# One quarter of the last block's gate by half products beside another stage, and three row sums by negated copies and DMA

## The chip, the cores and the metric

The kernel runs on one core of a Trainium2 chip. The metric is the device time of one execution in microseconds. Three runs of the kernel before gave 201.1, 200.7 and 201.03, a median of 201.03. The profile is of one execution; times within it count from its first instruction, and its span goes to the last one.

## The reference

A sequence of 2048 tokens of width 512 is normalized, and two branches of the normalized sequence are added to the input: a diagonal state space model with 512 complex states, and a gated unit of width 1792.

```python
xn  = (x - mean(x)) / sqrt(var(x) + 1e-5)              # x: [1, 2048, 512], bf16
Bu  = einsum("bld,pd->blp", xn, B_bar)                 # 512 complex states
h_t = Lam_bar * h_(t-1) + Bu_t                         # a scan over the 2048 tokens
A   = 2 * einsum("blp,dp->bld", h, C).real + xn * Dskip
Bo  = (silu(xn @ w1) * (xn @ w3)) @ w2                 # w1, w3: [512, 1792], w2: [1792, 512]
out = x + A + Bo
```

## The kernel before

**Blocks, chunks, pairs.** The 2048 tokens are four blocks (0 to 3) of 512, each of four chunks of 128. Two chunks of a block are a pair; pairs 0 to 7 run through the blocks, so pair 4 is the first half of block 2, pair 5 its second half, pairs 6 and 7 are block 3. TensorE is given its work in a fixed order: gate and up projections of a block (`glu`, and `glu_last` for block 3), the state inputs (`bu`, or `bu_fast` by half products), and the output products of the pairs (`y_fast`).

**The activation tile.** `act(b)` holds for each chunk of a block the left operands of the output product, fp16, as 22 slices of 128x128: 14 products silu(gate) * up, and 8 slices of states. The first 11 (`NK`) are the first seven gate slices and the states of the first half of the state space, the other 11 the rest. A pair thus has four quarters `a11`, `a12` (its first chunk) and `a21`, `a22` (its second).

**Seven products for eight.** `y_fast(n)` computes the two output chunks of a pair with Strassen's seven products in Winograd's form, each eleven matmuls of 256 columns (L1054). Its left operands are the quarters and four sums, made by `row_sums(n)`: `s3 = a11 - a21`, `s2 = s3 - a22`, `s1 = a21 + a22` (in place of `a21`) and, inside `y_fast`, `s4 = a12 + s2` (in place of `a12`, L1093 by an accumulating transfer that GpSimd issues, or L1096 by VectorE). `s2` and `s3` have homes in old tiles: for even pairs in the first two blocks of `x_all`, for odd ones in the last quarter of `tw`. The order of the products of pair 4 is 1, 4, 2, 6, 5, 7, 3. Product 3, which reads `s4`, is put off for the pairs in `LATER`: for pair 4 it runs inside pair 5, behind product 5, and for pair 5 inside pair 6.

`glu_last(3)` takes the 14 feature slices of block 3 so: slices 12 and 13 first, plainly; then three groups (`NG`) of four slices. In a group the up projection is computed by seven products (`product`, L869: four matmuls of 256 columns each) whose left operands are quarters of `w3` and their sums over weights (`up_sums`, `ups`), and whose right operands are quarters and column sums of the block's normalized input (`t1` to `t4`). The gate projection is computed plainly by `gate_side` (L848: four matmuls of 512 columns for a slice), four of these to a group, set between the products. Of a group's PSUM tiles two are `ps_y` banks (`g`, `e`) and two `ps_bu` banks (`f`, `z`); each of the two pools has two banks. ScalarE copies one running sum into the next bank (L857) and `silu`s the gate sides (L860); VectorE adds the copied product `s5` to two of the quarters (L879); each pair of slices ends with silu(gate) * up on VectorE (L864). The sum `s4` of each group is made on VectorE at L910.

**VectorE's queue.** The work that need not stand at a fixed place is queued in `Filler`: each task has a planned cost, the planner keeps a planned time for TensorE (`tensor`) and for VectorE, and `fill` issues tasks while VectorE's planned time plus half of the next task's cost is within TensorE's planned time plus a lead (1.7). `own` books fixed work. `flush(key)` issues everything up to the last task with that key. `y_fast` opens with flushes: its own pair's sums, and, for the first pair of block 2 or 3, the scans of the next block's first half:

```python
        bg.flush(("sums", n))
        bg.flush("tw")
        bg.flush(("difference", b))
        if p == 0 and b > 1:
            bg.flush(("scan", b + 1))
```

The queue at the point of the change holds, in this order, the rest of block 2's state products, block 3's products ahead of its scans (`pre_a`, `pre_b`, `pre_c` for each half), pair 4's row sums, the four scans of block 3's first half (`scans0`, L505), and what follows from these. `pre_c` adds a product to the state input: on VectorE at L493, or by an accumulating transfer at L495.

Instructions on one engine run in the order in which the program issues them, and GpSimd (POOL) issues the accumulating transfers in its own order.

Of the kernel before, what the change touches and what calls it, by code (L numbers as in the profile page):

```python
# [63 lines left out]
def kernel(  # L64
# [31 lines left out]
    NG = 3  # L96
    TH = TBLK // 2
    LEAD = 1.7
    LATER = (4, 5)
    AHEAD = (MID, 8, 1, None)  # L100
    NWARM = 10
    DH = D // 2
# [359 lines left out]
    def ssm_tasks(b, posts_last=False, between=(), middle=(), late=()):  # L462
# [5 lines left out]
        def half(hf):  # L468
            psl = slice(2 * hf, 2 * hf + 2)
            st = {}  # L470

            def pre_a():
                if b == 0:
                    sin_step((2 * hf + 1, 1))
                    nc.vector.tensor_scalar(out=tabe[:, psl, 2, :], in0=tabe[:, psl, 1, :], scalar1=-1.0,
                                            scalar2=None, op0=ALU.mult)
                st["g"] = u_blk[b, hf]
                if (b, hf) == (3, 0):
                    st["p"] = up.tile(FULL, BF16, name="u")
                elif b == NBLK - 1:  # L480
                    st["p"] = xtp.tile([P, NDT, TBLK], BF16, name="xnT").rearrange("p (j r) t -> p j r t", r=2)
                else:
                    st["p"] = ssmw.tile(FULL, BF16, name="p")
                nc.vector.tensor_tensor(out=st["p"][:, :, ::-1, :], in0=st["g"], in1=tabe[:, psl, 2:0:-1, :],
                                        op=ALU.mult)

            def pre_b():
                nc.vector.tensor_tensor(out=st["g"], in0=st["g"], in1=tabe[:, psl, 0:1, :].to_broadcast(FULL),  # L488
                                        op=ALU.mult)

            def pre_c():
                if b == 0 or (b, hf) == (2, 0):
                    nc.vector.tensor_tensor(out=st["g"], in0=st["g"], in1=st["p"], op=ALU.add)  # L493
                else:
                    gp.dma_start(out=st["g"], in_=st["p"], accum_op=ALU.add)  # L495

            def scan(j, ri):
                pt = 2 * hf + j
                init = 0.0
                if b in (1, 2):  # L500
                    init = ends[:, hf, 2 * j + ri:2 * j + ri + 1]
                elif b > 2:
                    init = act_blk[b - 1][:, CPB - 1, k_state(pt, ri), P - 1:P]
                v = st["g"][:, j, ri, :]
                nc.vector.tensor_tensor_scan(out=v, data0=rho[:, pt:pt + 1].to_broadcast([P, TBLK]), data1=v,  # L505
                                             initial=init, op0=ALU.mult, op1=ALU.add)

            def post_a(csl=slice(0, CPB)):
                if "p16" not in st:
                    st["p16"] = ssmw.tile(FULL, BF16, name="p").bitcast(FP16).rearrange(  # L510
                        "p j r (c t) -> p (j r c t)", t=P).rearrange("p (c k t) -> p c k t", c=CPB, t=P)
                tsl = slice(csl.start * P, csl.stop * P)
                nc.vector.tensor_tensor(out=by_state(st["p16"][:, csl]), in0=by_chunk(st["g"][:, :, ::-1, tsl]),  # L513
                                        in1=by_chunk(tabe[:, psl, 2:0:-1, tsl]), op=ALU.mult)

            def post_b(csl=slice(0, CPB)):
                tsl = slice(csl.start * P, csl.stop * P)
                n = csl.stop - csl.start
                nc.vector.tensor_tensor(out=by_state(act_state(b, hf)[:, csl]), in0=by_chunk(st["g"][:, :, :, tsl]),  # L519
                                        in1=by_chunk(tabe[:, psl, 0:1, tsl]).to_broadcast([P, 2, 2, n, P]), op=ALU.mult)  # L520

            def post_c(csl=slice(0, CPB)):
                a, p16 = act_state(b, hf)[:, csl], st["p16"][:, csl]
                if b == NBLK - 1 and (hf == 1 or csl.start > 0):
                    nc.vector.tensor_tensor(out=a, in0=a, in1=p16, op=ALU.add)
                else:
                    gp.dma_start(out=a, in_=p16, accum_op=ALU.add)  # L527

            if (b, hf) == (1, 1):
                pre_c.ready = lambda: ("squares", 2, CPB - 1) in sins_done  # L530
            pre_a.ready = lambda: (b, hf) in u_blk
            scans = [lambda j=j, ri=ri: scan(j, ri) for j in range(2) for ri in range(2)]
            return (pre_a, pre_b, pre_c), scans, (post_a, post_b, post_c)

        (pre0, scans0, post0), (pre1, scans1, post1) = (half(hf) for hf in range(NPT // 2))

        transfers = (post0[2],) + (() if b == NBLK - 1 else (post1[2],)) + ((pre1[2],) if b > 0 else ()) + ((pre0[2],) if b in (1, 3) else ())

        def add(*fns):
            for fn in fns:  # L540
# [285 lines left out]
    def up_sums(b):  # L826
# [8 lines left out]
                for out, x, z, op in ((s1, a21, a22, ALU.add), (s3, a11, a21, ALU.subtract),  # L835
                                      (s2, s1, a11, ALU.subtract))]

    def glu_last(b):
        xnT = xnT_blk[b]
        s1, s2, s3, s4 = ups["s"]  # L840
# [33 lines left out]
        def halves(ps):  # L874
            return ps.rearrange("p (h t) -> p h t", h=2)

        def add(out, ps):
            bg.own(0.7)
            nc.vector.tensor_tensor(out=out, in0=halves(ps), in1=halves(s5), op=ALU.add)  # L879

        gates = []
        for f in range(4 * NG, NFT):
            if f % 2 == 0:
                tiles = pair_tiles()
            gate_side(f, tiles[0])
            copy(tiles[1][:, f % 2, :], side(w3_sb, f))
            bg.fill()
            if f % 2 == 0 and gates:
                gates.pop()()
            if f % 2 == 1:  # L890
                gates.append(lambda f=f, tiles=tiles: gate(f - 1, tiles))
        for n in range(NG):
            f0 = 4 * n
            a11, a12, a22, s1n, s2n, s3n, s4n = (v[:, :, n, :] for v in (
                up_quarter(0, 0), up_quarter(1, 0), up_quarter(1, 1), s1, s2, s3, s4))
            g, e = (ps_y.tile([P, TBLK], FP32, name="y_ps") for _ in range(2))
            f, z = (ps_bu.tile([P, TBLK], FP32, name="bu_ps") for _ in range(2))
            upper, lower = pair_tiles(), pair_tiles()
            product(g, a11, b11, True)
            copy(f, g)  # L900
            product(e, s1n, t1, True)
            copy(s5, e)
            gate_side(f0, upper[0])
            bg.fill(0.8)
            gates.pop()()
            product(f, a12, b21, False)
            product(g, s2n, t2, False)
            copy(e, g)
            bg.own(0.42)
            nc.vector.tensor_tensor(out=s4n, in0=a12, in1=s2n, op=ALU.subtract)  # L910
            copy(upper[1][:, :, 0:TH], halves(f))
            gate_side(f0 + 1, upper[0])
            bg.fill()
            product(g, s3n, t3, False)
            copy(z, g)
            add(lower[1][:, :, TH:TBLK], g)
            product(e, s4n, b22, False)
            add(upper[1][:, :, TH:TBLK], e)
            gate_side(f0 + 2, lower[0])
            bg.fill()  # L920
            gate(f0, upper)
            product(z, a22, t4, False)
            copy(lower[1][:, :, 0:TH], halves(z))
            gate_side(f0 + 3, lower[0])
            bg.fill()
            gates.append(lambda f0=f0, lower=lower: gate(f0 + 2, lower))
        seeds(4)
        return gates.pop()


    def res_list(b):
# [56 lines left out]
        return [[v[:, 0:n] for v in xs], [spare[:, 0:n], spare[:, n:2 * n]]], q  # L988

    sums = {}  # L990

    def row_sums(n, b, p):
        a = act(b)
# [5 lines left out]
        def subtract(out, x, z):  # L999
            return lambda: nc.vector.tensor_tensor(out=out, in0=x, in1=z, op=ALU.subtract)  # L1000

        three = (0.84, subtract(s3, a11, a21), ("sums", n))
        two = (0.84, subtract(s2, s3, a22), ("sums", n))
        if n in (1, 6, 7):
            one = (0.84, lambda: nc.vector.tensor_tensor(out=a21, in0=a21, in1=a22, op=ALU.add), ("sums", n))
        else:
            one = (0.0, lambda: gp.dma_start(out=a21, in_=a22, accum_op=ALU.add), ("sums", n))
# [28 lines left out]
    def y_fast(n, then=(), between=()):  # L1036
# [50 lines left out]
        def product2():  # L1087
# [9 lines left out]
            add(o1[:, D1], f, o1[:, D1])  # L1097
            if last:
                store(c1, o1, D1)
            if n + 1 < len(pairs) and n not in (1, 2, 3) and n - 1 not in LATER:  # L1100
                seeds(n + 1)
            steps()

# [43 lines left out]
        for i in ((1, 5, 2, 6, 4, 3, 7) if b == 0 else (1, 2, 4, 6, 5, 7, 3) if b == 1 else ORDER.get(n, (1, 4, 2, 6, 5, 7, 3))):  # L1147
# [10 lines left out]
            if between:  # L1158
# [2 lines left out]
                    bg.fill()  # L1161
                if n == 3 and not between:
                    bg.first(up_sums(3))
            if n == 2 and i == 7:
                seeds(3)

    ln_alloc(0)
    ln1a, ln1b = ln_tasks_vector(1)
# [70 lines left out]
    y_done.append(2)  # L1239
    y_fast(3, (), bu_fast(3, 1))  # L1240
    bg.flush("up")
    gate = glu_last(3)
    gate()
    for n in range(4, len(pairs)):
        ahead = row_sums(n + 1, *pairs[n + 1]) if n + 1 < len(pairs) else ()
        if n > 4:
            for t in ahead:
                bg.add(*t)
        if n == 5:
            for t in (difference(3), *last_posts):  # L1250
                bg.add(*t)
        y_fast(n, ahead if n == 4 else ())


# [28 lines left out]
```

## Time and profile before

| | |
|---|---|
| median of three runs | 201.03 us (200.7 to 201.1) |
| span of the profiled execution | 199.5 us |
| TensorE matmuls busy | 195.6 us (98%), 1401 instructions |
| VectorE busy | 181.8 us (91%), 254 instructions |
| ScalarE busy | 135.0 us (68%), 281 instructions |
| GpSimd busy | 51.5 us (26%), 75 instructions |
| `glu_last(3)` on TensorE | 140.05 to 163.10 us |
| pairs 4 and 5 on TensorE, with product 3 of pair 4 but not of pair 5 | 163.10 to 178.71 us |
| pairs 6 and 7, with product 3 of pair 5 | 178.71 to 196.79 us |

The page gives the profiled execution's span and no separate time for it. Busy time is per engine; an engine that is busy all the time is the bound only where the others wait for it. The chain of waits follows the execution back from its last instruction, and the timeline lists one engine's instructions by start, with the duration and, in brackets, the idle time before one and what ended it. Durations of neighbouring instructions overlap a little, so the distance between two starts is the better measure of what an instruction adds.

### The profile page before, as it was taken

Reading aid. Unit: us, or ns where it says so; the run is one execution under the profiler, and the core shown is the slowest. Engines: PE = TensorE matmul, PEld = TensorE weight load, DVE = VectorE, ACT = ScalarE, POOL = GpSimd, SP = SyncE. Lnnn points to the kernel's source line nnn. Section 1 sums busy time; section 2 is a strip of 40 time slices with the busy share of each in tenths; the row PEclk is TensorE's granted clock in tenths of the full one; section 3 lists DMA queues with packets and bytes.
Section 4 is the critical chain, followed back from the end, with each engine's and each line's share of the span. In section 5 each row is a group of like instructions: output and inputs, shape, how many; then the busy total and the mean of one; then the engine's idle time right before and its main releaser. Section 6 shows DMA issues by size and latency. Waiting matters only on the chain.

```text
span 199.5 us, 3700 instructions
## 1 busy us (share of the span) xinstructions
PE 195.6 (98%) x1401; PEld 130.7 (65%) x1401; DVE 181.8 (91%) x254; ACT 135.0 (68%) x281; POOL 51.5 (26%) x75
## 2 busy tenths in 40 slices
PE   8999999999999999999999999999999999999994
PEld 2774444444444488866555468888566678888893
DVE  3689699999999999989999997999999999999972
ACT  4699897699999996968998684362588783111220
POOL 7180289700411134041202305040021303310000
PEclk9999999999999999999999999999999999999999
DMA  4999996991497054730997455838137732941111
GB/s 138 326 277 200 302 186 124 343 273 23 69 181 141 0 105 82 135 105 0 156 148 119 89 92 98 172 83 132 53 59 129 149 56 52 174 92 36 53 44 40
DMA packets 32258, 25.12 MB, mean 126 GB/s; under 512 B 16240, under 2 KB 29936, under 8 KB 32240
## 3 DMA queue, kind: packets, MB, share of 16 engines
q0 software_dynamic: 6128, 11.38, 33.5%
q1 hardware_dynamic: 25536, 13.21, 26.8%
q10 hardware_dynamic: 576, 0.30, 0.5%
q8 instruction: 11, 0.18, 0.4%
q14 instruction: 7, 0.06, 0.1%
HBM read 7.74 MB, written 2.10 MB: 49 GB/s over the span
## 4 chain that ended last, share of the span: by engine, by line
PE 95%; DMA 2%; SPq 1%; issue 0%; DVE 0%
PE gu_ps L587 34%; PE gu_ps L1054 17%; PE y_ps L1054 10%; PE gu_ps L848 7%; PE bu_ps L1054 7%; PE bu_ps L454 3%; PE y_ps L454 3%; PE y_ps L869 3%; PE y_ps L780 3%; DMA w_sb<-in_B_w_dram 2%; PE gu_ps L619 2%; PE gu_ps L780 2%; PE bu_ps L869 1%; PE bu_ps L780 1%; PE bu_ps L619 1%; SPq L166 0%
## 5 line engine op out<-in xcount | busy, mean ns | idle before, releaser
L587 PE MATMUL gu_ps<-xnT,w_sb 128*128 128x512 bf16 x312 | 69.6, 379 | 0.0
L587 PEld LDWEIGHTS <-w_sb 128*128 128x128 bf16 x312 | 30.5, 98 | 34.2
L1054 PEld LDWEIGHTS <-act 128*128 128x128 f16 x462 | 43.5, 98 | 5.4
L596 ACT ACTIVATE g<-gu_ps 128x512 bf16<-128x512 f32 x41 | 24.8, 606 | 6.0 <-PE gu_ps L587 3.6
L597 ACT ACTIVATE u<-gu_ps 128x512 bf16<-128x512 f32 x41 | 24.8, 606 | 4.5 <-PE gu_ps L587 3.7
L505 DVE TENSOR_TENSOR_SCAN u<-rho,ends,u 128x512 bf16<-128x512 f32 x16 | 20.0, 1270 | 0.0
L527 POOL DMA_DIRECT2D act<-p x7 | 9.2, 1320 | 34.0 <-DVE act L519 22.1
L1054 PE MATMUL gu_ps<-w_sb,act 128*128 128x256 bf16 (+3 forms) x126 | 16.0, 267 | 0.0
L848 PE MATMUL gu_ps<-xnT,w_sb 128*128 128x512 bf16 x64 | 15.9, 379 | 0.0
L604 DVE TENSOR_TENSOR act<-g,u 128x1024 f16<-128x1024 bf16 x21 | 14.2, 679 | 0.4 <-ACT u L597 0.4
L860 ACT ACTIVATE g<-gu_ps 128x512 bf16<-128x512 f32 x14 | 8.4, 599 | 5.4 <-PE gu_ps L848 5.0
L454 PEld LDWEIGHTS <-bt 128*128 128x128 bf16 x64 | 6.3, 98 | 7.5
L1077 ACT ACTIVATE x_blk<-gu_ps 128x256 f32<-128x256 f32 (+1 forms) x9 | 3.3, 368 | 10.6 <-PE gu_ps L1054 10.6
L1054 PE MATMUL bu_ps<-w_sb,act 128*128 128x256 bf16 (+3 forms) x84 | 10.4, 264 | 0.0
L1054 PE MATMUL gu_ps<-ct,act 128*128 128x256 f16 (+1 forms) x72 | 10.4, 267 | 0.0
L848 PEld LDWEIGHTS <-w_sb 128*128 128x128 bf16 x64 | 6.3, 98 | 4.8
L505 DVE TENSOR_TENSOR_SCAN u<-rho,u 128x512 bf16<-128x512 f32 x8 | 9.2, 1206 | 0.0
L1054 PEld LDWEIGHTS <-x_blk 128*128 128x128 f16 x88 | 8.6, 98 | 1.0
L1054 PEld LDWEIGHTS <-tw 128*128 128x128 f16 x88 | 8.6, 98 | 1.0
L513 DVE TENSOR_TENSOR p<-u,tabe 128x2048 f16<-128x2048 bf16 (+1 forms) x8 | 8.7, 1085 | 0.1
L519 DVE TENSOR_TENSOR act<-u,tabe 128x2048 f16<-128x2048 bf16 (+1 forms) x8 | 8.7, 1083 | 0.0
L488 DVE TENSOR_TENSOR u<-u,tabe 128x2048 bf16<-128x2048 bf16 x7 | 8.5, 1219 | 0.1
(203 smaller groups left out, 392.5 us busy)
## 6 DMA issues: line engine op xcount, KB each, us to landing
act<-p POOLq DMA_DIRECT2D x6, 512.0 KB, 6.1
xn<-x_blk POOLq DMA_DIRECT2D x4, 512.0 KB, 5.5
out_dram<-xn SPq DMA_DIRECT2D x15, 128.0 KB, 1.7
w_sb<-in_B_w_dram SPq DMA_DIRECT2D x1, 1792.0 KB, 8.2
act<-act POOLq DMA_DIRECT2D x5, 352.0 KB, 4.6
w_sb<-in_B_w_dram SPq DMA_DIRECT2D x2, 768.0 KB, 6.4
u<-p POOLq DMA_DIRECT2D x3, 512.0 KB, 5.1
w_sb<-in_B_w_dram SPq DMA_DIRECT2D x4, 256.0 KB, 4.9
```

Source lines behind the costliest of these rows:

```text
L454: nc.tensor.matmul(out=ps, lhsT=bt[:, ri, dt, pt * P:(pt + 1) * P], rhs=xnT_blk[b][:, dt, :], start=(dt == 0), stop=(dt == NDT - 1))
L505: nc.vector.tensor_tensor_scan(out=v, data0=rho[:, pt:pt + 1].to_broadcast([P, TBLK]), data1=v, initial=init, op0=ALU.mult, op1=ALU.add)
L513: nc.vector.tensor_tensor(out=by_state(st["p16"][:, csl]), in0=by_chunk(st["g"][:, :, ::-1, tsl]), in1=by_chunk(tabe[:, psl, 2:0:-1, tsl]) ...
L519: nc.vector.tensor_tensor(out=by_state(act_state(b, hf)[:, csl]), in0=by_chunk(st["g"][:, :, :, tsl]), in1=by_chunk(tabe[:, psl, 0:1, tsl] ...
L527: gp.dma_start(out=a, in_=p16, accum_op=ALU.add)
L587: nc.tensor.matmul(out=ps[:, tsl], lhsT=w[:, dt, f * P:(f + 1) * P], rhs=xnT[:, dt, tsl], start=(dt == 0), stop=(dt == NDT - 1))
L596: nc.scalar.activation(out=g16[:, f % 2, :], in_=g_ps, func=ACT.Silu)
L597: nc.scalar.activation(out=u16[:, f % 2, :], in_=u_ps, func=ACT.Copy)
L604: nc.vector.tensor_tensor(out=act_gates(b, f - 1), in0=split(g16), in1=split(u16), op=ALU.mult)
L780: nc.tensor.matmul(out=out[:, h * TH:(h + 1) * TH], lhsT=left[:, h, k, :], rhs=right[:, k, :], start=(start and h == 0 and k == 0), stop=( ...
L848: nc.tensor.matmul(out=ps, lhsT=w[:, dt, f * P:(f + 1) * P], rhs=xnT[:, dt, :], start=(dt == 0), stop=(dt == NDT - 1))
L1054: nc.tensor.matmul(out=out, lhsT=left[:, k, :], rhs=right[k][:, cols], start=(start and k == 0), stop=(k == NK - 1), skip_group_check=True)
```

## The change

For the third group of `glu_last(3)` (slices 8 to 11) the gate side is no longer computed by four plain projections set between the up side's products. It is computed by seven half products of its own, with the same right operands, and both sets of seven run beside pair 4: `glu_last` issues the up side's first two products and returns the rest as six steps, which `y_fast(4)` takes between its products. The gate side's left operands are quarters of `w1`; their five sums (`gate_sums`) are made on VectorE during groups 0 and 1, in the places of the first two groups' old sums, and the up side's own `s4` of that group with them. Where a gate quarter needs the added `s5`, VectorE adds it in the PSUM bank, and ScalarE's silu then reads the bank.

Three row sums, `s3` of pair 4 and `s3` and `s2` of pair 5, are no longer made on VectorE. ScalarE writes a negated copy of the second operand, and GpSimd issues a transfer that adds the first. `pre_c` of block 2's first half goes from VectorE to a transfer. Pair 4 leaves `LATER`, so its product 3 stands in its place in the order, and pair 5's PSUM tiles are seeded behind pair 4's product 7.

```diff
-    LATER = (4, 5)
+    LATER = (5,)
...
             def pre_c():
-                if b == 0 or (b, hf) == (2, 0):
+                if b == 0:
                     nc.vector.tensor_tensor(out=st["g"], in0=st["g"], in1=st["p"], op=ALU.add)
                 else:
                     gp.dma_start(out=st["g"], in_=st["p"], accum_op=ALU.add)
...
+    def gate_quarter(kh, r, half=False):
+        f0 = 4 * (NG - 1) * P
+        v = w1_sb[:, 2 * kh:2 * kh + 2, f0 + r * 2 * P:f0 + (r + 1) * 2 * P]
+        return v.bitcast(FP16) if half else v
+
+    def gate_sums():
+        s1, s2 = (ups["s"][i][:, :, 0, :] for i in range(2))
+        a11, a12, a21, a22 = (gate_quarter(*i) for i in ((0, 0), (1, 0), (0, 1), (1, 1)))
+        s3 = gate_quarter(0, 1, True)
+        u2 = ups["s"][1][:, :, NG - 1, :]
+        u4, s4 = (ups["s"][i][:, :, 1, :] for i in range(2))
+        ups["gs"] = a11, a12, a22, s1, s2, s3, s4
+        ups["u4"] = u4
+        return [(0.42, lambda out=out, x=x, z=z, op=op: nc.vector.tensor_tensor(out=out, in0=x, in1=z, op=op), "gs")
+                for out, x, z, op in ((s1, a21, a22, ALU.add), (s3, a11, a21, ALU.subtract),
+                                      (s2, s1, a11, ALU.subtract))], [
+            (0.42, lambda out=out, x=x, z=z: nc.vector.tensor_tensor(out=out, in0=x, in1=z, op=ALU.subtract), "gs")
+            for out, x, z in ((u4, up_quarter(1, 0)[:, :, NG - 1, :], u2), (s4, a12, s2))]
...
+        def group(lefts, four, top, low, gated):
+            a11, a12, a22, s1n, s2n, s3n, s4n = lefts
+            g, e = (ps_y.tile([P, TBLK], FP32, name="y_ps") for _ in range(2))
+            f, z = (ps_bu.tile([P, TBLK], FP32, name="bu_ps") for _ in range(2))
+
+            def end(out, ps):
+                nc.scalar.activation(out=out, in_=halves(ps), func=ACT.Silu if gated else ACT.Copy)
+
+            def add(out, ps):
+                bg.own(0.7)
+                nc.vector.tensor_tensor(out=halves(ps) if gated else out, in0=halves(ps), in1=halves(s5), op=ALU.add)
+                if gated:
+                    end(out, ps)
+
+            def one():
+                product(g, a11, b11, True)
+                copy(f, g)
+
+            def five():
+                product(e, s1n, t1, True)
+                copy(s5, e)
+
+            def two():
+                product(f, a12, b21, False)
+
+            def six():
+                product(g, s2n, t2, False)
+                copy(e, g)
+                four()
+                end(top[:, :, 0:TH], f)
+
+            def seven():
+                product(g, s3n, t3, False)
+                copy(z, g)
+                add(low[:, :, TH:TBLK], g)
+
+            def three():
+                product(e, s4n, b22, False)
+                add(top[:, :, TH:TBLK], e)
+
+            def last():
+                product(z, a22, t4, False)
+                end(low[:, :, 0:TH], z)
+
+            return one, five, two, six, seven, three, last
...
         gates = []
+        by_copy[4][0][0]()
...
-        for n in range(NG):
+        for n in range(NG - 1):
...
+            one()
+            five()
+            by_copy[5][0][n + 1]()
...
+            if n == 1:
+                bg.first(sums_b)
+                bg.flush("gs")
+            if n == 0:
+                sums_a, sums_b = gate_sums()
+                bg.first(sums_a)
         seeds(4)
-        return gates.pop()
...
+        one, five, two, six, seven, three, last = up_steps
+        gone, gfive, gtwo, gsix, gseven, gthree, glast = (gate_step(i) for i in range(7))
+        first = gates.pop()
+        return (one, five, by_copy[5][1][1], first), deque(((two, six, by_copy[5][1][2]), (seven, three), (last, gone, gfive), (gtwo, gsix),
+                                          (gseven, gthree), (glast, lambda: gate(f0, upper), lambda: gate(f0 + 2, lower))))
...
+        def from_copy(out, x, z, k0, k1, transfer):
+            nc.scalar.activation(out=out[:, k0:k1], in_=z[:, k0:k1], func=ACT.Copy, scale=-1.0)
+            if transfer:
+                gp.dma_start(out=out, in_=x, accum_op=ALU.add)
+
+        KH = (NK + 1) // 2
+        by_copy[n] = [[lambda v=v, r=r, k=k: from_copy(*v, *r, k) for r, k in (((0, NK), True), ((0, KH), False),
+                                                                              ((KH, NK), True))]
+                      for v in ((s3, a11, a21), (s2, s3, a22))]
...
+        if n in (4, 5):
+            three = (0.0, lambda: None, ("sums", n))
+        if n == 5:
+            two = (0.0, lambda: None, ("sums", n))
...
-            if n + 1 < len(pairs) and n not in (1, 2, 3) and n - 1 not in LATER:
+            if n + 1 < len(pairs) and n not in (1, 2, 3, 4) and n - 1 not in LATER:
                 seeds(n + 1)
...
-            if n == 2 and i == 7:
-                seeds(3)
+            if n in (2, 4) and i == 7:
+                seeds(n + 1)
...
-    gate = glu_last(3)
-    gate()
+    sums5 = row_sums(5, *pairs[5])
+    begin, beside = glu_last(3)
+    for step in begin:
+        step()
+        bg.fill()
...
-        y_fast(n, ahead if n == 4 else ())
+        y_fast(n, ahead if n == 4 else (), beside if n == 4 else ())
```

The steps of the up half keep the group's old names (`one` to `last`); those of the gate half are `gone`, `gfive`, `gtwo`, `gsix`, `gseven`, `gthree` and `glast`. `group` for the gate half is called with its first step, and so takes the PSUM banks that the up half has had.

## The prediction

> **What bounds the kernel now.** I read the page's chain of waits first, then that chain in order of time around the change, then VectorE's timeline over the same stretch, because an engine that is not the bound can still hold the one that is.
>
> ```profile
> PE 95%; DMA 2%; SPq 1%; issue 0%; DVE 0%
> ```
>
> TensorE is 95% of the chain. In order of time, the third tile group of block 3 (the one that the change touches) and the pair behind it, as start, duration and what ran:
>
> ```profile
> 156.56 0.87 PE y_ps L869 x8
> 157.43 0.86 PE gu_ps L848 x4
> 158.30 0.44 PE bu_ps L869 x4
> 158.73 0.44 PE y_ps L869 x4
> 159.17 0.86 PE gu_ps L848 x4
> 160.03 0.90 PE y_ps L869 x8
> 160.93 0.86 PE gu_ps L848 x4
> 161.80 0.44 PE bu_ps L869 x4
> 162.23 0.86 PE gu_ps L848 x4
> 163.10 7.21 PE gu_ps L1054 x66
> ```
>
> Every piece starts where the last one ended: TensorE waits for nobody here, so work taken from it shortens the run by its own size, provided that no wait appears. Four 512-column matmuls take 0.865 us (157.43 to 158.30), four 256-column ones 0.436 (0.87 for eight), and a product of a pair, eleven matmuls, 1.20 (7.21 for 66).
>
> VectorE over the same stretch:
>
> ```profile
> 154.83 1.29 DVE L879 TENSOR_TENSOR u<-y_ps,bt 128x512 bf16<-128x512 f32 x2 [0.31 <-ACT bu_ps L857]
> 156.03 0.88 DVE L1000 TENSOR_TENSOR x_blk<-act 128x1408 f16<-128x1408 f16 x1
> 156.83 0.68 DVE L864 TENSOR_TENSOR act<-g,u 128x1024 f16<-128x1024 bf16 x1
> 157.44 0.88 DVE L1000 TENSOR_TENSOR x_blk<-x_blk,act 128x1408 f16<-128x1408 f16 x1
> 158.24 0.68 DVE L864 TENSOR_TENSOR act<-g,u 128x1024 f16<-128x1024 bf16 x1
> 158.84 0.42 DVE L910 TENSOR_TENSOR w_sb<-w_sb,bt 128x512 f16<-128x512 bf16 x1
> 159.18 2.45 DVE L505 TENSOR_TENSOR_SCAN u<-rho,act,u 128x512 bf16<-128x512 f32 x2
> 161.55 1.26 DVE L879 TENSOR_TENSOR u<-y_ps,bt 128x512 bf16<-128x512 f32 x2
> 162.84 0.69 DVE L864 TENSOR_TENSOR act<-g,u 128x1024 f16<-128x1024 bf16 x1
> 163.45 1.28 DVE L505 TENSOR_TENSOR_SCAN u<-rho,act,u 128x512 bf16<-128x512 f32 x1
> 164.65 0.67 DVE L864 TENSOR_TENSOR act<-g,u 128x1024 f16<-128x1024 bf16 x1
> 165.23 1.28 DVE L505 TENSOR_TENSOR_SCAN u<-rho,act,u 128x512 bf16<-128x512 f32 x1
> ```
>
> VectorE is as full as TensorE: it goes from row to row without a gap, and it is late. The two adds of the third group (161.55) start 1.1 us after the product that the first of them reads has ended (160.03 + 0.44); that harms nobody here, since no matmul wants those PSUM banks soon. The four scans of block 3's first half are spread over 159.18 to 166.4, with the adds and gates between them. Starts differ by less than the durations, so I use start-to-start: 0.80 for a 1408-wide row sum, 0.60 for an add or a gate product, 0.34 for a 512-wide sum, 1.19 for a scan.
>
> **The change, part by part.** TensorE loses four gate sides, 4 x 0.865 = 3.46, and gains seven half products, 7 x 0.436 = 3.05: **-0.41 us**. All the rest is moved. If nothing waited, that would be the whole effect.
>
> VectorE loses the 2048-wide add of block 2 (1.14: 107.73 to 108.87 in its timeline), three row sums (3 x 0.80 = 2.40) and the third group's own sum (0.34); it gains five sums of the gate quarters (5 x 0.34 = 1.70) and two PSUM adds (2 x 0.60). Over the whole run that is -0.98, so VectorE as an average gets lighter. What matters is when.
>
> The block 2 add becomes a POOL transfer issued near 108. The like rows (L495) take 0.9 to 1.5 us on POOL and land 4.5 to 7.4 us after issue, so by 115.5; the scan that reads it stands at 121.58. On POOL it stands ahead of the residual transfer (111.23) and pair 2's row sum (113.05); a delay of that one by up to 3 us still lands by about 121, ahead of its product at 124.5. I price it at nothing; without that cover it would be up to 6 us on VectorE (7.4 less 1.14).
>
> The three row sums become ScalarE copies with a POOL accumulate. No row shows a 1408-wide copy. Bounds: 0.60 (a 512-wide one) and 1.96 (the 0.712 of a scaled 512-wide one times 2.75); the straight line through 0.38 at 256 and 0.60 at 512 gives 1.37, which I take, and 0.82 for the half of 768. The first fits into ScalarE's 2.6 us of idling before 140.95. A half beside group 0 starts the copy that frees PSUM for the next product some 0.1 late, against 0.2 of room (146.77 to 146.97): nothing, at worst 0.1. The Trainium skill, "ScalarE: Activation LUTs", section "Rules for kernel authors", speaks against this: such arithmetic belongs on VectorE. The same page's 186 + 0.833 N ns would make the copy 1.36 us by an estimate, as against 0.88 for the row sum; the sum here is the same by either, as ScalarE isn't on the path.
>
> The accumulates are 352 KB, as the row sums' own (0.86 on POOL, landing after 3.8 to 5.2). Pair 5's second waits on POOL for the first to land; behind it stands pair 4's fourth sum, a transfer that can start after its second product (162.8) and lands by 166.6 to 168.5. Pair 4's third product, no longer put off to pair 5, reads it at about 169.9. It costs nothing by that; the worst landing of such a tile in the trace, 9.1, would cost about 2.0, less whatever TensorE has already waited.
>
> **The wait that is new** is in the order. The gate half's products reuse the two ps_y banks of the up half's. The first of them may start only when VectorE's add in step `seven` has read the first bank, the second when the add in `three` has read the other. When does TensorE want them? From 156.56: one and five 0.87, pair product 1.20, two and six 0.87, pair product 1.20, seven and three 0.87, pair product 1.20, last 0.44: **163.21**.
>
> When is VectorE there? y_fast(4) opens by flushing pair 4's sums and block 3's four scans. Before, that call stood at 163.1 on TensorE and found only one scan left. Now it stands after two products of the third group, at 157.43, and all four scans are still queued: walking the queue's own arithmetic (limit TensorE + 1.7, next task's half cost) through groups 0 and 1, no scan is taken earlier. So all four are issued ahead of both adds. Start from 156.03, where the adds of group 1 end; their start, 154.83, is held by a ScalarE copy, so that the 1.14 saved at 107 is largely used up in such waits. Then the second row sum of pair 4 (0.80), two gates (1.20), the last two gate sums (0.68), four scans (2.37 x 2 = 4.74), the add (0.66 to its end): 156.03 + 0.80 + 1.20 + 0.68 + 4.74 + 0.66 = **164.11**. TensorE waits 0.90. The second bank is free 0.60 later, at 164.71, while `gone` ends at 164.55: another 0.16. **Stall 1.06**, and I take 1.1 with the tenth by which the copy ahead of group 1's adds is late.
>
> Bounds for the stall: if the saved 1.14 survives up to a row sum's worth, 0.3; if one more 2048-wide product of the queue (1.14) falls behind the adds at 154.83 and not into the 0.31 gap before them, 1.9. I take 1.1, since 154.83 is held from outside.
>
> Later the sum doesn't change: the nearest edge on VectorE behind is the last block's state add, which ends 189.37 before its product at 189.51, 0.14 of room. TensorE comes 0.7 later there and VectorE has two row sums fewer to do, so the room grows.
>
> **Sum.** The profiled execution's span is 199.5; the runs' median is 201.03, so 1.53 lies around the span, as I leave it. 199.5 - 0.41 + 1.1 = 200.2, and with 1.53 **201.7 us**. A difference of 0.2% (0.40 us) is about what a measurement of this kernel can tell from none.
>
> **Rivals.**
> - *No stall: 200.6.* 201.03 - 0.41. For it: VectorE's total falls by 0.98 and 1.14 of it well ahead. It decides if the four scans are through by 162.5, 0.9 earlier than I have them. Against it: the gaps at 148.3 and 154.8 are waits for ScalarE, which no lighter queue shortens. Even whole, it only just reaches 0.2%.
> - *Half a stall: 201.0.* VectorE arrives 0.7 ahead of my sum, the stall is 0.4 and eats the gain.
> - *A late transfer as well: 202.6.* Pair 4's fourth sum lands 9.1 after 162.8 and holds the third product for 0.9 beyond the 1.1. For it: two or three accumulates now share POOL's queue between 155 and 165. The Trainium skill, "DMA: Bandwidth & Descriptors", section "Two DMAs through the same engine are not ordered", has the issuing engine wait for the first one's completion; pair 5's second accumulate stands so on POOL. Against it: the two like rows with x_blk at 120.7 and 167.0 landed in 3.8, and the stall itself gives it a microsecond more.
>
> **How the numbers follow.** Stall 0.70, half 0.15, none 0.10, late transfer too 0.05. The stall's own range is 201.3 to 202.2 (0.7 to 1.6 of stall). For 8 in 10 I go down to 200.8, into the half case, and up to 202.5, the upper bound of the stall. Slower by over 0.2% needs a stall above 0.81: most of the first case and the last, less the edge: 0.70. Within 0.2%: 0.18. Faster: 0.12, the case without stall and its neighbours, as its middle lies on the edge.
>
> **What would show it.** The chain should have a gap or a DVE piece near 163 to 164, of about 1 us, ahead of the gate half's first product, with four scans in a row on VectorE before it; L869's matmuls 28 more, L848's 16 fewer; ScalarE copies of 1.3 to 1.4 us; pair 4's third product without a wait. I am wrong if TensorE goes through 157 to 172 without a gap, if the scans stand ahead of 158, or if a gap is elsewhere: in group 0's `three`, where the sum before it (146.36) may slip by up to 0.2, or ahead of pair 4's third product.

## The result and the profile after

The changed kernel takes 202.69 us (median of six runs, 202.28 to 203.26) against 201.06 (200.7 to 201.13) for the kernel before in the same comparison. The ratio is 1.0081, with a 95% interval of 1.0065 to 1.0096: **slower by 1.6 us**, where 201.7 with a range of 200.8 to 202.5 was forecast.

The page of the changed kernel, the line of the chain that was first read before:

```profile
PE 84%; DMA 6%; DVE 4%; ACT 2%; issue 1%; SPq 1%
```

TensorE was 95% of the chain. Transfers and VectorE now stand in it, so TensorE waits, and the chain in order of time says where (start, duration, what ran or was waited for):

```profile
132.16 0.76 DMA act<-p
132.91 6.57 DMA act<-tw
139.48 0.05 issue
139.52 1.38 PE bu_ps L1152 x11
...
159.70 4.72 DVE u L505 x4
164.43 0.59 DVE u L906
165.02 0.04 issue
165.06 1.19 PE y_ps L888 x8
```

There are two places. (Line numbers have moved: L1152 is the pair products' L1054, L888 the half products' L869, L906 the adds' L879, L1191 the fourth sum's transfer L1093.) The second is the wait of the prediction: four scans in a row, then the add, then the gate half's first product. The first place was not forecast: **pair 3's last product, well ahead of the changed stage, waits for a transfer**. TensorE's own timeline shows both, with the idle time in brackets:

```profile
137.77 1.36 PE L1152 MATMUL y_ps<-tw 128*128 128x256 f16 x11
139.52 0.94 PE L1152 MATMUL bu_ps<-w_sb,act 128*128 128x256 bf16 x7 [0.39 <-DMA act<-tw]
...
165.06 0.60 PE L888 MATMUL y_ps<-xnT,w_sb 128*128 128x256 bf16 x4 [0.93 <-DVE u L906]
165.66 0.60 PE L888 MATMUL y_ps<-x_blk,bt 128*128 128x256 f16 x4
```

A pair product is 1.20 us from start to start, so pair 3's third would have begun at 138.97: it is 0.55 late (the brackets count less, since the busy time of a matmul is drawn past the next one's start). By the timeline, where the third group's first product starts at 157.31, the gate half's first would have started 6.65 us behind it (the forecast's 163.21 less 156.56), at 163.96: it is 1.10 late. The second starts 0.60 behind the first where the next set follows after 0.44 in a running sequence, another 0.16. So 1.26 is lost there. (On the chain the same loss falls into other parts, because in a running sequence the chain places a product 0.16 behind its start in the timeline, and behind a wait it doesn't: 157.47 + 6.65 = 164.12, so 0.94 for the wait, and 0.32 for the two products, 1.19 in place of 0.87.)

From the first product of pair 3 to the start of VectorE's last instruction, on the chain, the kernel before takes 68.23 us (128.58 to 196.81) and the changed one 69.68 (128.87 to 198.55): +1.45, against -0.41 + 0.55 + 1.26 = 1.40. What lies ahead of pair 3 differs by 0.29 in these two executions. The first load of weights takes 4.95 and 4.53 us on the chain, and part of that difference is made good just behind it. Pair 3 starts anywhere between 128.10 (e5) and 129.08 (e1) in the profiles of the changed kernel and of its variants below, so this start is scatter, and all that follows counts from pair 3.

VectorE at the end of group 1, then where the adds come:

```profile
155.74 1.29 DVE L906 TENSOR_TENSOR u<-y_ps,bt 128x512 bf16<-128x512 f32 x2 [0.31 <-ACT bu_ps L876]
156.94 0.88 DVE L1085 TENSOR_TENSOR x_blk<-x_blk,act 128x1408 f16<-128x1408 f16 x1
157.74 0.69 DVE L883 TENSOR_TENSOR act<-g,u 128x1024 f16<-128x1024 bf16 x1
158.34 0.76 DVE L854 TENSOR_TENSOR bt<-w_sb,bt 128x512 f16<-128x512 bf16 x2
159.01 0.69 DVE L883 TENSOR_TENSOR act<-g,u 128x1024 f16<-128x1024 bf16 x1
159.62 4.81 DVE L505 TENSOR_TENSOR_SCAN u<-rho,act,u 128x512 bf16<-128x512 f32 x4
164.34 1.27 DVE L906 TENSOR_TENSOR u<-y_ps,bt 128x512 bf16<-128x512 f32 x2
```

These are the terms of the forecast sum, one by one: a row sum, a gate, two gate sums, a gate, four scans, the adds.

### The profile page after: what moved, and what is told of

Its sections match the earlier page's. It is cut to its first block, busy times and chain, and to the rows that moved or that the text cites. A ratio compares the mean times of both kernels' runs of the same rounds, so it can differ in the third digit from the quotient of the medians.

```text
span 201.3 us, 3737 instructions
## 1 busy us (share of the span) xinstructions
PE 195.3 (97%) x1400; PEld 132.3 (66%) x1413; DVE 180.7 (90%) x256; ACT 140.4 (70%) x290; POOL 55.3 (27%) x79
## 4 chain that ended last, share of the span: by engine, by line
PE 84%; DMA 6%; DVE 4%; ACT 2%; issue 1%; SPq 1%
PE gu_ps L587 33%; PE gu_ps L1152 16%; PE y_ps L1152 8%; PE bu_ps L1152 6%; PE bu_ps L454 3%; PE y_ps L454 3%; PE gu_ps L867 3%; DMA act<-tw 3%; PE y_ps L780 3%; DMA w_sb<-in_B_w_dram 2%; PE y_ps L888 2%; DVE u L505 2%; PE gu_ps L619 2%; PE bu_ps L780 1%; PE bu_ps L888 1%
## 5 line engine op out<-in xcount | busy, mean ns | idle before, releaser
L587 PE MATMUL gu_ps<-xnT,w_sb 128*128 128x512 bf16 x304 | 68.9, 379 | 0.4
L587 PEld LDWEIGHTS <-w_sb 128*128 128x128 bf16 x312 | 30.5, 98 | 34.2
L1152 PEld LDWEIGHTS <-act 128*128 128x128 f16 x462 | 43.5, 98 | 5.8 <-DMA act<-tw 0.7
L596 ACT ACTIVATE g<-gu_ps 128x512 bf16<-128x512 f32 x41 | 24.8, 606 | 6.2 <-PE gu_ps L587 3.3
L527 POOL DMA_DIRECT2D act<-p x7 | 9.1, 1306 | 38.6 <-DVE act L519 24.2
L1152 PE MATMUL gu_ps<-w_sb,act 128*128 128x256 bf16 (+3 forms) x126 | 16.0, 267 | 0.0
L867 PE MATMUL gu_ps<-xnT,w_sb 128*128 128x512 bf16 x45 | 11.5, 379 | 0.1
L1152 PE MATMUL bu_ps<-w_sb,act 128*128 128x256 bf16 (+3 forms) x84 | 10.4, 264 | 0.4 <-DMA act<-tw 0.4
L1152 PE MATMUL gu_ps<-ct,act 128*128 128x256 f16 (+1 forms) x72 | 10.4, 267 | 0.0
L888 PEld LDWEIGHTS <-w_sb 128*128 128x128 bf16 (+1 forms) x72 | 7.0, 98 | 3.9 <-issue 1.3
L1152 PEld LDWEIGHTS <-x_blk 128*128 128x128 f16 x88 | 8.6, 98 | 1.0
L1152 PEld LDWEIGHTS <-tw 128*128 128x128 f16 x88 | 8.6, 98 | 1.0
L879 ACT ACTIVATE g<-gu_ps 128x512 bf16<-128x512 f32 x10 | 6.0, 599 | 3.6 <-PE gu_ps L867 3.1
```

The costliest lines, as they stand in the source:

```text
L587: nc.tensor.matmul(out=ps[:, tsl], lhsT=w[:, dt, f * P:(f + 1) * P], rhs=xnT[:, dt, tsl], start=(dt == 0), stop=(dt == NDT - 1))
L596: nc.scalar.activation(out=g16[:, f % 2, :], in_=g_ps, func=ACT.Silu)
L867: nc.tensor.matmul(out=ps, lhsT=w[:, dt, f * P:(f + 1) * P], rhs=xnT[:, dt, :], start=(dt == 0), stop=(dt == NDT - 1))
L888: nc.tensor.matmul(out=out[:, h * TH:(h + 1) * TH], lhsT=left[:, k, h * P:(h + 1) * P], rhs=right[:, k, :], start=(start and h == 0 and k ...
L1152: nc.tensor.matmul(out=out, lhsT=left[:, k, :], rhs=right[k][:, cols], start=(start and k == 0), stop=(k == NK - 1), skip_group_check=True)
```

## The experiments

Each kernel is the changed one with the edit shown, if nothing else is said. The kernel before ran beside them: 201.21 us in the batch of e1 to e4, 201.0 in that of e5 to e8.

**e1: the order of block 2, by the planner's booking.** The added transfer of block 2 is booked as if VectorE still did the work, so that the queue's order is that of the kernel before.

```diff
-((pre0[2],) if b > 0 else ())
+((pre0[2],) if b in (1, 3) else ())
```

> The changed kernel with one thing altered: the planner goes on booking 1.16 us for block 2's addition to its state input, which is still a transfer. VectorE's order is then that of the kernel before up to block 3, and on POOL pair 3's fourth sum is issued ahead of block 2's state transfer again. Theory (the order on POOL made pair 3's third product wait 0.55 us): that wait is gone, the transfer lands about 3.8 us after issue and not 6.6; the wait of the gate half's first product (1.1 + 0.16) stays, since the four scans still stand ahead of both adds. Time 0.4 to 0.7 us under the changed kernel, about 202.1. Rival (the transfer was late because the queues carry more accumulates in all): the wait at pair 3's third product stays, 202.7.

Measured: 204.29 us, ratio 1.0164 (1.013 to 1.0199). Neither number came. Pair 3's wait is gone, as the theory has it, but the gate half's grew. TensorE's timeline:

```profile
165.85 1.01 PE L888 MATMUL y_ps<-xnT,w_sb 128*128 128x256 bf16 x4 [2.07 <-DVE u L906]
166.66 1.06 PE L888 MATMUL y_ps<-x_blk,bt 128*128 128x256 f16 x4
167.51 2.24 PE L1152 MATMUL gu_ps<-tw,x_blk 128*128 128x256 f16 x11
```

and VectorE's ahead of it, from the adds of group 1 on:

```profile
155.39 1.29 DVE L906 TENSOR_TENSOR u<-y_ps,bt 128x512 bf16<-128x512 f32 x2 [0.31 <-ACT bu_ps L876]
156.60 1.22 DVE L488 TENSOR_TENSOR x_blk<-x_blk,tabe 128x2048 bf16<-128x2048 bf16 x1
...
160.41 4.80 DVE L505 TENSOR_TENSOR_SCAN u<-rho,act,u 128x512 bf16<-128x512 f32 x4
```

With 1.16 more on the planner's account the queue is one task behind, and a 2048-wide product (156.60) falls behind the adds of group 1 where it stood ahead of them in the changed kernel. So the scans begin 0.8 later (160.41 for 159.62) with TensorE 0.35 earlier. This is the case of the prediction's upper bound for the stall, 1.9; the first bank alone came to 2.1 on the chain. And the products behind the wait are slow: eleven matmuls take 2.24 where 1.36 is the rule. The windows of this profile (stretch, its length, then the busy time of TensorE, its weight loads, VectorE, ScalarE and POOL, the granted clock, DMA share and GB/s) show why:

```profile
163.00:165.00 2.00, 0.78 (x8) 0.55 (x6) 2.00 (x2) 0.60 (x1) 0.97 (x2) 1.00 1.02 180
165.00:167.00 2.00, 1.15 (x6) 0.82 (x6) 1.72 (x4) 0.10 (x1) 0.86 (x1) 0.72 1.02 180
167.00:169.00 2.00, 2.00 (x11) 1.34 (x10) 0.00 (x0) 1.08 (x2) 0.00 (x0) 0.50 1.06 189
```

After the wait the granted clock falls to 0.50. The profiled execution is the slowest of the six (205.82 us). From pair 3 on it takes 72.04 us, 3.81 over the kernel before, of which 2.1 is the wait, some 1.8 the slow matmuls and the second bank behind it, and 0.3 waits in pairs 6 and 7, less 0.41. So e1 shows that pair 3's wait follows the order, and by missing its forecast that the stall at the gate half hangs on one task of the queue.

**e2: the scans not flushed ahead of the adds.** Two scans then stand ahead of the adds and two behind; no other instruction of VectorE or POOL changes its place.

```diff
-        if p == 0 and b > 1:
+        if p == 0 and b > 1 and n != 4:
             bg.flush(("scan", b + 1))
...
-            if b > 0:
+            if b > 0 and n != 4:
                 bg.first(list(then))
...
+                if n == 4 and len(between) == 3:
+                    bg.flush(("scan", b + 1))
+                    bg.first(list(then))
```

> The changed kernel with one thing altered: y_fast(4) doesn't flush the four scans at its start; two of them come behind the two adds of the up half, and pair 5's first row sum goes out behind them. Theory (the flushed scans hold the adds that free the two banks): the wait of 1.1 + 0.16 us at the gate half's first two products is gone, and with it 1.2 to 1.4 us: 201.3 to 201.5; pair 3's wait of 0.55 us stays. Rival (VectorE is short of time there by its added sums, whatever the order): TensorE waits about as long at a later place, 202.3 or more.

Measured: 201.28, ratio 1.0007 (0.9994 to 1.0019), as the theory had it. The wait is gone and nothing took its place: 68.47 from pair 3 on, 1.21 less than the changed kernel, with pair 3's wait left.

**e3: e1 and e2 together.**

> Both alterations of e1 and e2 together. If the two waits are the whole loss, TensorE runs from the first product to the last without a gap, and the removed matmul time comes out: 201.06 - 0.41 = 200.65, between 200.5 and 200.9 and under the kernel before. If the changed kernel loses by something else too (its first 13 us took 0.29 us more in its profile), 200.9 to 201.2.

Measured: 201.05, ratio 0.9998 (0.9986 to 1.0011); not told apart from the kernel before. The first expectation missed; the number of the second came, but not for its reason, since the loss stands at the end and not in the first 13 us. Both waits are gone, and 68.21 from pair 3 on is 0.26 less than e2 where 0.55 was to come. Who waits, for whom, in all, how often and the longest, by its view of the waits of weight loads:

```profile
PEld L1152 <- DVE act L525: 0.3, 2, 0.2
...
PEld L1152 <- DVE tw L1085: 0.2, 1, 0.2
PEld L1152 <- DVE x_blk L1085: 0.2, 1, 0.2
```

These are pairs 6 and 7 waiting for block 3's last state sums and their row sums; on the chain their stretches are 6.15, 2.46 and 1.29 long for 6.00, 2.40 and 1.20, 0.30 in all. TensorE, no longer late, has caught up with VectorE.

**e4: the transfer alone.** The kernel before, with the two lines of `pre_c` and of its booking, and no other part of the change.

```diff
-                if b == 0 or (b, hf) == (2, 0):
+                if b == 0:
...
-((pre0[2],) if b in (1, 3) else ())
+((pre0[2],) if b > 0 else ())
```

> The kernel before with one part of the change alone: block 2's addition to its state input becomes a transfer, booked at nothing. Theory (the order on POOL): block 2's state transfer is issued ahead of pair 3's fourth sum, that lands 6 to 7 us after issue, pair 3's third product waits about 0.55 us, and since VectorE is not the bound nothing is won: 201.5 to 201.7. Rival (this transfer is harmless by itself, as the prediction had it): 201.0 to 201.1, or a little less.

Measured: 201.54, ratio 1.002 (1.0009 to 1.0031), so 0.2 to 0.6 us slower. Pair 3's third product again comes late, by 0.58 (139.07, with the product ahead of it at 137.29). This part alone makes the kernel slower, though it takes 1.14 us of work from an engine that is 91% busy.

**e5: the order on POOL alone.** Block 2's first state transfer is put off until pair 3's fourth sum is issued.

```diff
+                elif (b, hf) == (2, 0) and 3 not in fourth:
+                    behind.append(lambda: gp.dma_start(out=a, in_=p16, accum_op=ALU.add))
...
                 gp.dma_start(out=v["s4"], in_=v["s2"], accum_op=ALU.add)
+                fourth.add(n)
+                while n == 3 and behind:
+                    behind.pop(0)()
```

> The changed kernel with one thing altered: POOL issues block 2's first state transfer behind pair 3's fourth sum, and nothing else moves, neither in VectorE's order nor in the planner. Theory (the order on POOL is the cause of pair 3's wait): that wait of 0.55 us is gone, VectorE keeps its lead, the wait of the gate half's first products stays at 1.1 + 0.16 us: 202.0 to 202.3. Rival, after e1: TensorE only arrives earlier at the gate half and waits there longer by as much: 202.5 to 202.8.

POOL's timelines about this place, of the kernel before (L1093 is the fourth sum, L527 the state transfer):

```profile
132.16 0.86 POOL L1093 DMA_DIRECT2D act<-tw  x1 [8.85 <-PE bu_ps L1054]
132.93 1.41 POOL L527 DMA_DIRECT2D act<-p  x1
```

of the changed kernel (L1191 is the fourth sum):

```profile
132.16 1.29 POOL L527 DMA_DIRECT2D act<-p  x1 [9.44 <-PE bu_ps L1152]
132.91 1.45 POOL L1191 DMA_DIRECT2D act<-tw  x1
```

and of e5 (L1194 and L528):

```profile
131.68 0.86 POOL L1194 DMA_DIRECT2D act<-tw  x1 [9.72 <-PE bu_ps L1155]
132.21 1.64 POOL L528 DMA_DIRECT2D act<-p  x1
```

Measured: 202.15, ratio 1.0052 (1.0035 to 1.0069), as the theory had it: 0.5 less than the changed kernel's 202.69. From pair 3 on it takes 69.12, so 0.56 less than the changed kernel, and the gate half's wait is the same 0.93 in brackets. Two transfers change places: the smaller (352 KB; the other has 512 KB) lands 6.6 us after issue when it is second (the changed kernel) and 3.8 to 3.9 when it is first (the kernel before and e5).

**e6: both orders, the planner as in the change.** The edits of e2 and e5.

> The changed kernel with both orders mended and the planner as in the change: POOL's as in e5, the scans' as in e2. Theory: no wait is left, neither at pair 3 nor at the gate half nor, as VectorE keeps the 1.14 us that e3's planner gave away, at pairs 6 and 7 (0.30 us in e3). From the first product of pair 0 to the end 0.41 us less than before, 126.4 us as against 126.8, and a median 0.3 to 0.5 under the kernel before. Rival (VectorE is the bound near the end): the waits at pairs 6 and 7 stay at 0.2 to 0.4 and the median is within 0.2 of the kernel before.

Measured: **200.5, ratio 0.9974 (0.9962 to 0.9986)**, faster than both kernels. 67.91 us from pair 3 on, 0.32 less than before: the 0.41, less two places of 0.05 (the second bank at the gate half, and group 0's third product, which takes 0.95 with its neighbour where 0.89 was). The medians differ by 0.5, with an interval of 0.3 to 0.8, so the profile's 0.32 is within what they allow. Pairs 6 and 7 don't wait. VectorE at the gate half:

```profile
158.54 2.45 DVE L506 TENSOR_TENSOR_SCAN u<-rho,act,u 128x512 bf16<-128x512 f32 x2
162.03 1.29 DVE L909 TENSOR_TENSOR u<-y_ps,bt 128x512 bf16<-128x512 f32 x2 [1.04 <-ACT bu_ps L879]
163.24 0.41 DVE L1166 TENSOR_TENSOR xn<-gu_ps,xn 128x256 bf16<-128x256 f32 x1
163.57 2.45 DVE L506 TENSOR_TENSOR_SCAN u<-rho,act,u 128x512 bf16<-128x512 f32 x2
```

The adds now wait for their products by way of ScalarE's copy (1.04 of idling), not for scans, and the last two scans stand where nobody needs VectorE at once.

**e7: the three row sums back on VectorE, in e6.**

```diff
-        by_copy[4][0][0]()
...
-            by_copy[5][0][n + 1]()
...
-        if n in (4, 5):
-            three = (0.0, lambda: None, ("sums", n))
-        if n == 5:
-            two = (0.0, lambda: None, ("sums", n))
```

(The two later calls of `by_copy` are taken out of the steps as well.)

> e6 with the three row sums back on VectorE, without the ScalarE copies and their transfers. Theory (VectorE has no room at the end: 0.14 us before): its 2.4 us more make pairs 6 and 7 wait for their left operands, by 0.5 to 1.5 us in all: 201.3 to 202.3. Rival (the copies were not needed): no wait, the time of e6.

Measured: 204.23, ratio 1.0164 (1.0145 to 1.0183). The direction is the theory's and the size is not: 3.7 us over e6 where 0.8 to 1.8 were expected. Pairs 6 and 7 wait for block 3's state sums, as here in pair 6 on TensorE, and twice more in pair 7 (1.6 in all):

```profile
181.27 0.61 PE L1149 MATMUL gu_ps<-tw,act 128*128 128x256 f16 x4 [1.33 <-DVE act L526]
```

VectorE idles 0.82 ahead of 174.40 and 1.27 ahead of 186.81 in that kernel, waiting for TensorE's products while tasks are still queued behind, so it loses more than its added 2.4; which order of the queue would avoid that wasn't tried.

**e8: e2 with the addition of block 2 back on VectorE.**

```diff
-                if b == 0:
+                if b == 0 or (b, hf) == (2, 0):
...
-((pre0[2],) if b > 0 else ())
+((pre0[2],) if b in (1, 3) else ())
```

> e2 with block 2's addition to its state input back on VectorE, so no part of that edit is left; POOL's order is then that of the kernel before. Compared with e3, which has the same order but the addition as a transfer. Theory (of the 1.14 us saved at 107 most is lost in waits further on): within 0.2 us of e3, with pairs 6 and 7 waiting 0.3 to 0.6 us: 201.0 to 201.4. Rival (the saved time reaches the end): 0.8 us or more slower than e3.

Measured: 201.2, ratio 1.0006 (0.9994 to 1.0018), 68.20 from pair 3 on against e3's 68.21. The 1.14 us of work on VectorE make no difference that these runs can tell if the queue's order stays: from 90 us on, the instructions of VectorE and of POOL follow in the same order in e3 and e8, but for that addition. In e6, where the planner knows of the saving and moves tasks forward, it is worth 0.30 (68.21 less 67.91).

## Why the prediction was wrong, and what of it held

*The bound and the saving* held. TensorE without waits gives back what the matmuls cost: e6 has 0.32 of the 0.41.

*The new wait* held in its place, its cause and its releaser: four scans flushed ahead of two adds, shown by e2, which moves two scans and takes 1.21 us away. The sum of VectorE's terms was 7.55 us from the third group's first product to the end of the first add (164.11 less 156.56); it measured 7.55 as well (165.02 less 157.47), and term by term. The second bank's 0.16 came too. The mis-sized term is the first bank's wait: 0.90 was forecast, 1.10 measured. The forecast took TensorE's times from the chain, and the timeline has the same products starting 0.16 earlier (157.31 for 157.47), so TensorE wanted the bank at 163.96 where the chain's reckoning gives 164.12; the other 0.04 is the piece called issue between the add and the product. 1.26 in all, against 1.06 worked out and 1.1 taken. The tenth that was added to 1.06 had another reason, a late copy ahead of group 1's adds, and that did not come: these adds start 1.73 ahead of the third group in both kernels.

*The step that failed* is that of block 2's addition: "I price it at nothing". It looked at what stands behind the new transfer on POOL, and there nothing was late. The cost came from the other side of the edit. Booked at nothing, the addition lets the planner issue later tasks of VectorE earlier. At pair 3, two state products of block 2 change places with a scan. VectorE before:

```profile
128.96 1.27 DVE L505 TENSOR_TENSOR_SCAN u<-rho,ends,u 128x512 bf16<-128x512 f32 x1
130.27 1.23 DVE L513 TENSOR_TENSOR p<-u,tabe 128x2048 f16<-128x2048 bf16 x1
131.41 1.22 DVE L519 TENSOR_TENSOR act<-u,tabe 128x2048 f16<-128x2048 bf16 x1
```

and in the changed kernel:

```profile
129.25 1.22 DVE L513 TENSOR_TENSOR p<-u,tabe 128x2048 f16<-128x2048 bf16 x1
130.38 1.22 DVE L519 TENSOR_TENSOR act<-u,tabe 128x2048 f16<-128x2048 bf16 x1
131.51 1.28 DVE L505 TENSOR_TENSOR_SCAN u<-rho,ends,u 128x512 bf16<-128x512 f32 x1
```

With the products the program issues their transfer earlier too: POOL had it behind pair 3's fourth sum, and now has it ahead. e4 shows that this part alone costs the time, e5 that the order of the two on POOL is the cause. It cost 0.55 us, and is what put the result outside the range, whose upper end was the stall's alone: without it, in e5, the time is 202.15.

*The walk of the queue* was right for the changed kernel and more fragile than its range said: by one task (e1) the stall is 2.1 us and the clock's fall comes on top. The upper bound of 1.9 had the mechanism, without the clock.

*The row sums by copy* cost next to nothing, as forecast: the 1408-wide copy takes 1.37 us, as the straight line had it, the halves 0.73 to 0.85, their transfers land in 3.7 to 3.8, and pair 4's third product doesn't wait. The two places of about 0.05 in e6 are gone in e7, which has no copies: group 0's third product takes 0.89 with its neighbour there and not 0.95, within the "at worst 0.1", and the gate half's first two products 0.87 and not 0.92. What they are worth (e7, 3.7 us) was not asked in the prediction, only that VectorE had 0.14 us of room at the end. That this room would grow held for the changed kernel, since TensorE is late in it; in e3, where it is not, 0.30 is lost there.

*The rivals.* The late transfer was priced at another place (pair 4's fourth sum, behind pair 5's second accumulate, where 5 in 100 were given) and came at pair 3's, by a shift of places which no rival had. Its price also rested on a misread row: the landing of 9.1 us is that of a 512 KB state transfer (L527), and the 352 KB transfers of the profile before landed in 3.8 to 5.2; 162.8 + 5.2 is 168.0, not 168.5. Pair 4's fourth sum, issued at 163.99, landed in 4.4.

Of the 1.63 us between the medians, 1.45 stands in the two profiles from pair 3 on; the rest is not settled (the end of this document has what is known of it).

## What to carry to other kernels

Work that is taken from an engine with a planned queue can move everything behind it: list, for each queue that the later tasks feed, which two transfers or instructions change places, and price that, before calling the saving free. A flush that is called at a new place does at once all that was spread out before; ask which banks the instructions behind it set free, and when they are wanted. Where TensorE has no gap, a change that saves 0.4 us needs its waits counted to a tenth: both of the waits here were larger than the saving, and with both orders mended the same edits are 0.26% faster than the kernel before.

## What was not expected of the hardware

**A wait of two microseconds can halve the clock behind it.** In the profiled execution of e1 TensorE idled 2.07 us in a row and was then granted 0.50 of its clock for 3.4 us, from about 165.9 to 169.3. By the mean clock it happened in three of the six runs (0.991, 0.991 and 0.992; 205.82, 204.73 and 205.15 us), and not in the others (1.0; 203.84, 203.40 and 203.69): 1.5 us between the medians of the two. In the changed kernel, with 0.93 of idling, and in e7, with 1.33, no run shows it (mean clock 0.998 or more). The Trainium skill, "TensorE: Matmul & The Clock Gate", section "Part 1: The HAM clock gate (the "warmup" mystery)", gives half rate after an idle window of about 3.4 us, and says that the window runs free of the kernel. That half of the runs are hit agrees with a free-running window, and the half clock lasted as long as one. The length of idling does not agree, since 2.1 us were enough here, and the measurement decides. How much of a window has to be idle no run here shows.

**Time outside the span.** The median of run time less span is 1.98 to 2.01 us in the three kernels that keep the four scans ahead of the adds (the changed one, e1, e5), and 1.76 to 1.87 in all others, the kernel before among them. Nothing else that sets the two groups apart was found in the profiles, and e7, whose waits are as long, is in the second. What these 0.2 us are stays open.
